# Keys, queries and attention outputs turned by DMA transposes instead of TensorE, in a fused attention and feed-forward kernel

## The chip, the cores and the metric

The kernel runs on one core of a Trainium2 chip. The core has a matrix engine (TensorE, PE in the profile, with its weight loads as PEld), a vector engine (DVE), a scalar engine (ACT), a general engine (POOL), a queue processor that issues most of the transfers (SP), and 16 DMA engines that carry them. The metric is the device time of one execution in microseconds, and the time of a kernel is the median of its runs.

## What is computed

Inputs are float32: `q`, `k`, `v` of shape (8 batches, 8 heads, 576 tokens, 64), 16 "beacon" keys and values for each batch and head that stand ahead of the others, and two weight matrices of 512 x 2048 and 2048 x 512. The reference, cut to what matters:

```python
k_all = np.concatenate([beacon_k, k], axis=2)          # 592 keys
v_all = np.concatenate([beacon_v, v], axis=2)
scores = scale * np.matmul(q, k_all.transpose(0, 1, 3, 2))
causal[:, Nb:] = np.triu(np.ones((S, S), dtype=bool), k=1)   # beacons are always seen
a = softmax(np.where(causal, -1e9, scores))
attn_out = np.matmul(a, v_all)                          # (B, H, S, D)
x = attn_out.transpose(0, 2, 1, 3).reshape(B * S, H * D)     # 4608 x 512
h = x @ w_in
g = np.where(h > 0.0, h, np.exp(np.minimum(h, 0.0)) - 1.0)   # elu
out = g @ w_out                                         # 4608 x 512, float32
```

## The kernel before

**Attention** runs batch by batch and, within a batch, over four pairs of heads (`n` counts pairs, 32 in all). Keys and queries of a pair come from HBM as one tile `st32` (L266): a partition holds nine consecutive tokens of one head, keys on the even partitions and queries on the odd ones, so that a row of the transfer is 9 x 64 floats. POOL or DVE casts the tile to bfloat16 (`cast_pair`, L275). The matmul needs the 64 features on the partitions, so TensorE turns the tile with nine transposes of 128 x 128 and one for the beacon keys (`do_T`, L310) into the PSUM tile `tr`, which shares the two buffers of tag `sc` with the scores. DVE copies the keys out of it in token order (`do_kT`, L322) and ACT or DVE the queries (`do_qT`, L327).

Scores are made transposed, keys on the partitions (`do_SC`, L334), in chunks of 128 keys (`NKC`, 5) and three ranges of queries (0 to 240, 240 to 496, 496 to 576; `CUT`, L183). The last range is padded so that its last chunk is 128 columns wide (L168). ACT takes the exponential (`do_exp`, L346), POOL masks the diagonal parts (`do_mask`), TensorE multiplies with `v` (`do_AV`, L364), and DVE divides by the row sum (`do_norm`, L380), which gives `x16`, tokens on the partitions. The feed-forward needs x with its 512 columns on the partitions: TensorE transposes each pair's five blocks (`do_xT`, L395), and DVE copies the result to `xT` (`do_xcopy`, L404).

**The feed-forward** runs over tiles of 512 tokens (the first is cut in two): 16 first matmul steps (`do_mm1`, L418: `hps`), elu over ACT (`do_e`), POOL (`do_clamp`) and DVE (`do_join`, giving `gt`), 16 second steps (`do_mm2`, L445: `ops`), a copy `osb` on DVE and a store. Each step is four matmuls of 128 x 512. A tile needs the x of all the batches that its tokens come from.

**Loads.** SP issues nearly all of them. `v` comes by tokens, 128 tokens on the partitions and rows of 64 floats (L280), and is cast by DVE into `v16`. Weights come in 32 pieces through buffers of tag `gt`, which later hold the elu's results.

**The order.** `Plan` (L27) is a list scheduler that runs when the kernel is built. Each operation has an engine, a key (its due time), an assumed duration, the operations it depends on and the buffers it takes and gives back. The planner goes through time and starts on each engine the ready operation with the smallest key; on TensorE none that is due more than 16 us after the earliest one left. Instructions are written in that order, so on the chip each engine's order is fixed and only the waits move. `place(b, a)` (L477) gives the due times of batch b with 32 us from one batch to the next; `SHIFT`, `AT`, `AT0`, `PACES`, `LAG` and `URGE` are hand-set due times, `FIRST` the order of the first loads, `ON_POOL` and `Q_ON_ACT` say which engine casts and copies. SP's loads are chained one behind the other in key order (L639); stores take their place by due time.

Of the kernel before, what the change touches and what calls it, by code (L numbers as in the profile page):

```python
# [27 lines left out]

# [85 lines left out]
def kernel(  # L119
# [43 lines left out]
    class Cut:  # L163
        def __init__(self, ranges, splits):
            self.ranges, self.parts, self.units, self.of_range = ranges, [], [], []
            for (lo, hi), split in zip(ranges, splits):
                part = [(jc, max(lo, first_q[jc]), hi - max(lo, first_q[jc])) for jc in range(NKC) if first_q[jc] < hi]
                if hi == S:  # L168
                    part[-1] = (part[-1][0], part[-1][1], P)
                self.parts.append(part)  # L170
                self.of_range.append(list(range(len(self.units), len(self.units) + len(split))))
                for chunks in split:
                    self.units.append([p for p in part if p[0] in chunks])
# [14 lines left out]
    SQP = BLOCKS[-1][0] + P  # L188
# [20 lines left out]
    NG, NET, NKQ = 20, 8, 4  # L209
# [16 lines left out]
    xT = [big.tile([P, NT], FP16, name=f"xT{cc}") for cc in range(NCC)]  # L226
# [4 lines left out]
    kTs = [big.tile([P, SKP], BF16, name=f"kT_{i}") for i in range(NKQ)]  # L231
    qTs = [big.tile([P, SQP], BF16, name=f"qT_{i}") for i in range(NKQ)]
# [3 lines left out]
    with tc.tile_pool(name="psum", bufs=1, space=bass.MemoryType.PSUM) as psum:  # L236
        slots = {
            "sc": 2, "ff": 4, "av": 2, "ops": 1, "et": NET, "rl": 2, "e": NE, "gt": NG, "osb": 3,
            "st": 4, "sb": 2, "bk": 1, "vst": 5,
# [14 lines left out]
        issues = []  # L254

        bks = {}

        def load_bk(b):
            t = bks[b] = stage.tile([P, DM], FP32, tag="bk", name="bk32", bufs=1)
            nc.sync.dma_start(  # L260
                out=t[0:NB].rearrange("n (h d) -> n h d", h=H), in_=beacon_k[b].rearrange("h n d -> n h d"))
# [17 lines left out]

        def load_v(b, jc):  # L280
            vst = vsts[b, jc] = stage.tile([P, H, D], FP32, tag="vst", name="vst", bufs=5)
# [28 lines left out]
        def do_T(n):  # L310
            b, hp = divmod(n, HP)
            tr = trs[n] = psum.tile([P, 2 * 1024], BF16, tag="sc", name="tr", bufs=2)
            for g in range(G):
# [3 lines left out]
                out=tr[:, P * G:P * G + NB], in_=bk16s[b % 2][0:NB, P * hp:P * hp + P], identity=identb[0:NB, 0:NB])  # L317
# [9 lines left out]
        def do_qT(n, eng):  # L327
            out, in_ = qTs[n % NKQ][:, 0:S].rearrange("c (p g) -> c p g", g=G), in_order(n, 1)
            if eng is nc.scalar:
                eng.activation(out=out, in_=in_, func=AFT.Copy)  # L330
            else:
                eng.tensor_copy(out=out, in_=in_)
# [14 lines left out]
        def do_exp(n, u):  # L347
            w = CUT.width[u]
            et = ets[n, u] = attn.tile([P, 2, 512], FP16, tag="et", name="et", bufs=NET)
# [12 lines left out]
        def do_AV(n, groups):  # L362
# [3 lines left out]
            for i, blk in enumerate(blocks_of(groups)):  # L366
                q0, rows, nk = BLOCKS[blk]
                for h in range(2):
                    c = (2 * i + h) * VW
                    for jc in range(nk):  # L370
# [8 lines left out]
                            start=(jc == 0), stop=(jc == nk - 1), skip_group_check=True)  # L379
            avs[n, groups[0]] = av  # L380
# [77 lines left out]
        def do_store(tt, t4):  # L458
# [5 lines left out]
        SHIFT = [3.37, -1.96, 6.24, 4.57, 2.84, -4.23, 2.71, 5.78]  # L464
        AT = [6.55, -0.8, -0.58, -0.4, -1.02, 0.94, 2.18]
        AT0 = [[-30.36, -35.31, -37.63, -37.29], [-37.9, -27.04, -33.24, -32.64], [-16.09, -15.68, -1.02, 2.44]]
        PACES = [(-17.79, 2.03, 18.97, 2.42), (-2.78, 3.03, 40.86, 0.57), (35.62, 1.7, 18.91, 3.41), (71.48, 2.79, 36.3, 3.28), (111.77, 1.64, 28.1, 2.06)]
        ON_POOL = ("1101011100110100", "1111111110110110", "01001010")
        LAG = 20.58
        URGE = 13.63  # L470
        Q_ON_ACT = "11111110"
        FIRST = (
            "k0 q0 b0 q1 i3 v0 k1 q2 k3 v2 i8 k2 q3 v1 v3 i0 i7 i4 i11 i15 i10 v4 i9 i2 i5 i1 i13 b1 k4 "
            "i6 i14 q4 i12 v5 o2 o5 o3 o8 o0 o6 o7 v6 q5 k5 o1 o4 o9 v9 k6 v8 q6 o12 v7 o14 o10 q7 o11 "
            "o15 o13 k7 ").split()
# [6 lines left out]
        scaled, last_xT = {}, {}  # L482
# [8 lines left out]
        def plan_loads(n):  # L491
            b, hp = divmod(n, HP)
            if hp == 0:
                got = load(load_key(f"b{b}", place(b, 0) - 31), 0.2, partial(load_bk, b), take=["bk"])
                bk_in[b] = add("POOL", place(b, -0.9), 0.6, partial(cast_bk, b),
                               deps=[got, last_T.get(b - 2)], give=["bk"])
# [11 lines left out]
        def plan_v(b):  # L508
            for jc in range(NKC):
                key = load_key(f"v{NKC * b + jc}", place(b - 1, 1.8 + 0.4 * jc))  # L510
                got = load(key, 1.25, partial(load_v, b, jc), take=["vst"], issue=1.0 if jc == 0 else 0.5)
# [9 lines left out]
        def plan_pair(n):  # L521
# [3 lines left out]
            T = add("PE", key, 0.6, partial(do_T, n),  # L525
# [4 lines left out]
            if Q_ON_ACT[b] == "1":  # L530
                qT = add("ACT", key + 0.4 - URGE, 0.7, partial(do_qT, n, nc.scalar), deps=[T, last_kq.get(n - NKQ)])
            else:
                qT = add("DVE", key + 0.5 - URGE, 0.77, partial(do_qT, n, nc.vector), deps=[T, last_kq.get(n - NKQ)])
            add("NONE", key, 0.0, None, deps=[kT, qT], give=["sc"], lat=0.0)
            masked = {}
# [3 lines left out]
            for units, key in steps:  # L539
                SC = add(  # L540
                    "PE", key, sum(0.00024 * 2 * CUT.width[u] + 0.02 for u in units), partial(do_SC, n, units),
                    deps=[kT, qT, SC], take=["sc"] * len(units), mode=1, lat=0.19)
                last_kq[n] = SC
# [12 lines left out]
            for r, groups in enumerate([(0,), (1,), (2,)] if b == 0 else [(0,), (1, 2)]):  # L556
# [10 lines left out]
                    deps=[AV, last_xT.get(n - 2 * HP)], give=["ff", "av"]))  # L567
                if b and r == 0:
                    continue
                if b:  # L570
                    groups, key = (0, 1, 2), at(AT[6])
                blks = blocks_of(groups)
# [11 lines left out]
        def plan_tile(p):  # L584
# [3 lines left out]
            for b in range(B):  # L588
                for r, (rlo, rhi) in enumerate(CUT.ranges):
                    if b * S + rlo < hi and b * S + rhi > lo:  # L590
                        xs += [scaled[b * HP + hp, r] for hp in range(HP)]
# [31 lines left out]
        for t in kTs:  # L623
            nc.vector.memset(t[:, SK:SKP], 0.0)
        for t in qTs:
            nc.vector.memset(t[:, S:SQP], 0.0)
# [5 lines left out]
        for b in range(B):  # L632
            plan_v(b)
            for hp in range(HP):
                plan_loads(b * HP + hp)
# [35 lines left out]
```

## Time and profile before

| | |
|---|---|
| median of 3 runs | 378.2 us (376.53 to 382.88) |
| profiled execution | 377.09 us, its span 375.4 us |
| granted TensorE clock | 0.999 |
| TensorE busy | 355.5 us |
| DVE, ACT, POOL busy | 231.7, 205.5, 199.9 us |
| HBM read and written | 37.22 and 9.44 MB |

The profile is one execution. The span runs from its first to its last instruction; the execution's own time is 1.7 us longer. The busy time of an engine is the sum of its instructions' durations without overlap. Matmuls are pipelined, and their ends are modelled: two neighbours overlap in the rows of the timeline, and the start of one to the start of the next is what a step takes. In the lists a row names the engine, the line of the kernel (L314), the operation, what it writes and reads, and the count. "SPq" rows are DMA issues on SP's queue; a DMA row gives the size and the median time from issue to landing.

Where the change is made, the page counts these operations: 288 transposes of keys and queries (L314) and 32 of beacon keys (L316) on TensorE; 32 key copies (L324) of 756 ns in the mean and 32 small ones (L325) of 156 on DVE; 28 query copies on ACT (L330) of 650 ns and four on DVE (L332) of 748; 160 transposes of x (L400) on TensorE, and 40 copies of x (L407) on DVE, of which 28 are 128 x 576 at 455 ns; 27 casts of pairs on POOL (L277) at 1148 ns and five on DVE at 808.

### The profile page before, as it was taken

The page shows a single profiled execution, that of the slowest core. Times are in us where ns is not written, and L with a number is a line of the kernel's source. Part 1 is how long each engine was busy: PE and PEld are TensorE (multiplying, and loading weights), DVE is VectorE, ACT ScalarE, POOL GpSimd, SP SyncE. Part 2 cuts the span into 40 slices and gives each one's busy share as a digit, 9 for nine tenths or more (in the row PEclk, how much of TensorE's full clock was granted, in tenths as well). Part 3 has the DMA queues.
Part 4 walks back from the last instruction along what each step waited for, and adds up shares of the span by engine and source line. Part 5 has one row for each costly group of instructions (what it writes and reads, how often), then busy time and mean ns, then how long its engine had stood idle before and what let it go on. Part 6 is the DMA issues. An engine that isn't in the chain of part 4 may idle for free.

```text
span 375.4 us, 8560 instructions
## 1 busy us (share of the span) xinstructions
PE 355.5 (95%) x3360; PEld 199.7 (53%) x3360; DVE 231.7 (62%) x489; ACT 205.5 (55%) x301; POOL 199.9 (53%) x369
## 2 busy tenths in 40 slices
PE   1598999999999999999999999999999999999995
PEld 1367766645556555555655455554655544444442
DVE  2469798668657867668847645666765645555321
ACT  2566767568857767887654455655563333333100
POOL 3459998467846755766744535546343333433200
PEclk9999999999999999999999999999999999999999
DMA  7999999992363467293272420000000000100021
GB/s 186 277 324 322 298 314 248 318 246 93 92 174 100 141 151 177 86 255 97 66 203 74 110 75 30 30 28 30 31 31 28 30 28 28 56 30 28 30 91 76
DMA packets 58855, 47.21 MB, mean 126 GB/s; under 512 B 41920, under 2 KB 41920, under 8 KB 58816
## 3 DMA queue, kind: packets, MB, share of 16 engines
q1 hardware_dynamic: 58672, 46.38, 43.1%
q8 instruction: 26, 0.43, 0.5%
q10 hardware_dynamic: 144, 0.29, 0.2%
q14 instruction: 13, 0.11, 0.1%
HBM read 37.22 MB, written 9.44 MB: 124 GB/s over the span
## 4 chain that ended last, share of the span: by engine, by line
PE 81%; DMA 8%; SPq 3%; DVE 3%; POOL 2%; ACT 1%; issue 1%; ACTq 0%; DVEq 0%
PE ops L450 32%; PE hps L423 30%; PE av L375 6%; PE sc L341 6%; DMA wst<-in_moe_w_in_dram 4%; DMA vst<-in_v_dram 3%; PE tr L314 3%; PE xt L400 2%; SPq L300 1%; DMA st<-in_q_dram 1%; POOL w_out L305 1%; POOL e L433 1%; DVE gt L442 1%; PE tr L316 1%; SPq L287 1%
## 5 line engine op out<-in xcount | busy, mean ns | idle before, releaser
L450 PE MATMUL ops<-w_out,gt 128*128 128x512 f16 x576 | 144.4, 379 | 0.0
L423 PE MATMUL hps<-xT,w_in 128*128 128x512 f16 (+1 forms) x640 | 143.7, 358 | 0.1
L433 POOL TENSOR_SCALAR e<-e 128x512 f32<-128x512 f32 x144 | 89.2, 621 | 98.6 <-ACT e L429 97.9
L429 ACT ACTIVATE e<-hps 128x512 f32<-128x512 f32 x144 | 85.8, 600 | 92.5 <-PE hps L423 89.2
L442 DVE SCALAR_TENSOR_TENSOR gt<-e,hps 128x512 f16<-128x512 f32 x144 | 97.5, 683 | 59.4 <-POOL e L433 58.8
L350 ACT ACTIVATE et<-sc 128x736 f16<-128x736 f32 (+3 forms) x128 | 106.2, 884 | 23.0 <-PE sc L341 21.8
L423 PEld LDWEIGHTS <-w_in 128*128 128x128 f16 x640 | 59.1, 98 | 55.5 <-issue 1.4
L450 PEld LDWEIGHTS <-gt 128*128 128x128 f16 x576 | 51.8, 98 | 57.3 <-issue 2.7
L356 POOL TENSOR_SCALAR_AFFINE_SELECT et<-et 128x256 f16<-128x256 f16 (+2 forms) x160 | 60.8, 401 | 37.0 <-ACT et L350 34.4
L375 PEld LDWEIGHTS <-et 128*128 128x128 f16 (+1 forms) x960 | 37.1, 99 | 12.0 <-issue 3.5
L341 PE MATMUL sc<-qT,kT 64*128 64x80 bf16 (+3 forms) x704 | 37.9, 238 | 5.7 <-ACT qT L330 3.9
L375 PE MATMUL av<-v,et 128*128 128x65 f16 (+1 forms) x960 | 41.9, 195 | 1.0 <-DVE v L291 0.7
L456 DVE COPY osb<-ops 128x512 f32<-128x512 f32 x36 | 24.8, 689 | 24.3 <-PE ops L450 24.0
L324 DVE COPY kT<-tr 128x576 bf16<-128x576 bf16 x32 | 24.2, 756 | 19.2 <-PE tr L316 13.0
L277 POOL CAST st<-st 128x1152 bf16<-128x1152 f32 x27 | 31.0, 1148 | 8.5 <-PE tr L314 4.7
L330 ACT ACTIVATE qT<-tr 128x576 bf16<-128x576 bf16 x28 | 18.2, 650 | 29.1 <-DVE kT L325 18.1
L390 DVE TENSOR_TENSOR x<-av,rl 128x256 f16<-128x256 f32 (+2 forms) x68 | 32.1, 472 | 2.3
L341 PEld LDWEIGHTS <-kT 64*128 64x128 bf16 x704 | 22.0, 96 | 21.4 <-issue 10.6
L314 PE MATMUL tr<-identb,st 128*128 128x128 bf16 x288 | 23.2, 230 | 7.5 <-DVE st L277 6.0
L291 DVE CAST v<-vst 128x512 f16<-128x512 f32 (+1 forms) x40 | 22.2, 564 | 7.3 <-DMA vst<-in_v_dram 7.3
L314 PEld LDWEIGHTS <-st 128*128 128x128 bf16 x288 | 19.6, 103 | 12.9 <-DVE st L277 6.4
L389 DVE RECIPROCAL rl<-av 128x4 f32<-128x4 f32 (+2 forms) x68 | 12.4, 182 | 14.8 <-PE av L375 14.6
(25 smaller groups left out, 92.9 us busy)
## 6 DMA issues: line engine op xcount, KB each, us to landing
st<-in_k_dram SPq DMA_DIRECT2D x32, 288.0 KB, 3.5
out_dram<-osb SPq DMA_DIRECT2D x36, 256.0 KB, 2.0
st<-in_q_dram SPq DMA_DIRECT2D x31, 288.0 KB, 4.3
vst<-in_v_dram SPq DMA_DIRECT2D x24, 256.0 KB, 5.9
wst<-in_moe_w_in_dram SPq DMA_DIRECT2D x16, 256.0 KB, 6.6
wst<-in_moe_w_out_dram SPq DMA_DIRECT2D x16, 256.0 KB, 5.9
vst<-in_v_dram SPq DMA_DIRECT2D x8, 224.0 KB, 4.8
vst<-in_v_dram SPq DMA_DIRECT2D x8, 160.0 KB, 4.9
```

The source lines that it names most:

```text
L277: eng.tensor_copy(out=o.rearrange("p g h d -> p h g d"), in_=f32s[n].rearrange("p h (g d) -> p h g d", g=G))
L314: nc.tensor.transpose(out=tr[:, P * g:P * g + P], in_=b16s[n][:, g].rearrange("p h d -> p (h d)"), identity=identb)
L341: nc.tensor.matmul(out=sc[:, h, o:o + w], lhsT=kT[D * h:D * h + D, P * jc:P * jc + P], rhs=qT[D * h:D * h + D, q0:q0 + w], start=True, sto ...
L350: nc.scalar.activation(out=et[:, :, 0:w], in_=scs[n, u][:, :, 0:w], func=AFT.Exp, bias=0.0, scale=float(1.0 / (D ** 0.5)))
L356: nc.gpsimd.affine_select(out=et[:, :, c0:c0 + dw], in_=et[:, :, c0:c0 + dw], compare_op=ALU.is_ge, fill=fill0, base=q0 + NB - P * jc, pat ...
L375: nc.tensor.matmul(out=av[:, c:c + D + 1], lhsT=ets[n, CUT.unit_of[jc, at]][0:m, h, col:col + P], rhs=v16[0:m, jc, 2 * hp + h, 0:D + 1], s ...
L390: nc.vector.tensor_tensor(out=x16s[b % 2][:, blks[0]:blks[0] + nb, P * hp:P * hp + P].rearrange("q i (h d) -> q i h d", d=D), in0=av[:, :, ...
L423: nc.tensor.matmul(out=hps[:, (hi - lo) * j:(hi - lo) * (j + 1)], lhsT=w_in16[:, cc, P * fc:P * fc + P], rhs=xT[cc][:, lo:hi], start=(cc = ...
L429: nc.scalar.activation(out=e, in_=hpss[tt, i], func=AFT.Exp, bias=0.0, scale=1.0)
L433: nc.gpsimd.tensor_scalar(out=e, in0=e, scalar1=1.0, scalar2=0.0, op0=ALU.min, op1=ALU.max)
L442: nc.vector.scalar_tensor_tensor(out=gt, in0=es[tt, i], scalar=1.0, in1=hpss[tt, i], op0=ALU.subtract, op1=ALU.max)
L450: nc.tensor.matmul(out=ops, lhsT=gts[tt, fc][:, P * t4:P * (t4 + 1)], rhs=w_out16[:, fc, :], start=(fc == 0), stop=(fc == NFC - 1))
```

## The change

From batch 2 on (`PE_B = 2`) the path of keys and queries is another. `load_tok` loads them by tokens, as `v` is loaded: 128 tokens on the partitions, all eight heads in a row of 512, rows of the transfer 64 floats long; the beacon keys go ahead of chunk 0 of the keys. Two chunks share a buffer of tag `st`. `cast_tok` casts one or two chunks to bfloat16 on DVE or POOL, by the table `TOK`. `turn_tok` is a DMA transpose issued by SP, from the cast chunk in SBUF straight to the key or query tiles of all four pairs of heads, ten for each batch. These tiles are now one per batch and side, with two batches held (`kTa`, `qTa`). The scores of a pair wait for all ten transposes of their batch. TensorE's transposes, the copies from PSUM and the loads by pairs stay for batches 0 and 1.

For batches 1 to 7, x goes another way too: when all four pairs of a batch have a block of tokens in `x16`, `turn_x` transposes the block by DMA into `xT`, five for each batch. Batch 0 stays with TensorE and DVE.

Besides: the last range of scores isn't padded (its last chunk is 80 columns wide), and the eight `et` tiles are fixed buffers whose tail is cleared once by POOL; beacon keys are transposed with 128 rows; `v` staging has four buffers instead of five, shared with the beacon keys; the `gt` tag has 18 buffers instead of 20; more weight casts are on DVE; and due times, `FIRST` and the engine tables have new values.

```diff
-    NG, NET, NKQ = 20, 8, 4
+    NG, NET, NKQ = 18, 8, 2 * HP
+    PE_B = 2
...
-    kTs = [big.tile([P, SKP], BF16, name=f"kT_{i}") for i in range(NKQ)]
-    qTs = [big.tile([P, SQP], BF16, name=f"qT_{i}") for i in range(NKQ)]
+    kTa = [big.tile([P, HP, SKP], BF16, name=f"kT_{i}") for i in range(2)]
+    qTa = [big.tile([P, HP, S], BF16, name=f"qT_{i}") for i in range(2)]
...
+        TURN = 1.2
...
+        def load_tok(b, is_k, c):
+            if (b, is_k, c // 2) not in f32s:
+                f32s[b, is_k, c // 2] = stage.tile([P, 2, G * D], FP32, tag="st", name="st32", bufs=4)
...
+            nc.sync.dma_start(out=t[r0:r0 + n], in_=(k if is_k else q)[b, :, lo:lo + n, :].rearrange("h s d -> s h d"))
+
+        def cast_tok(b, is_k, c, m, eng):
+            o = b16s[b, is_k, c // 2] = stage.tile([P, G, 2, D], BF16, tag="sb", name="st16", bufs=2)
...
+        def turn_tok(b, is_k, c):
+            r0, n, lo = rows_of(is_k, c)
+            t = (kTa if is_k else qTa)[b % 2]
+            nc.sync.dma_start_transpose(
+                out=t[:, :, P * c:P * c + r0 + n],
+                in_=b16s[b, is_k, c // 2].rearrange("p g h d -> p (g h d)")[0:r0 + n, DM * (c % 2):DM * (c % 2) + DM])
+
+        def turn_x(b, blk):
+            q0, rows, _ = BLOCKS[blk]
+            nc.sync.dma_start_transpose(
+                out=xTa[:, :, b * S + q0:b * S + q0 + rows], in_=x16s[b % 2][0:rows, blk, :])
...
+        DMA_AT = [-22.53, -24.72, -12.02]
+        TOK = ("101010", "001000", "000101", "100000", "000111", "111110")
...
+        def plan_tok(b):
+            turned[b] = []
+            for is_k in (True, False):
+                for c in range(0, NKC, 2):
...
+                    for j in range(m):
+                        s = add("SP", place(b, DMA_AT[1]) + i, TURN, partial(turn_tok, b, is_k, c + j),
+                                deps=[cast, last_SC.get(b - 2)])
+                        turned[b].append(add("DMA", place(b, DMA_AT[1]) + i, 0.5, None, deps=[s],
+                                             give=["sb"] if j == m - 1 else [], lat=2.2))
...
+            ready = plan_copies(n) if b < PE_B else turned[b]
...
+                if b:
+                    for blk in blks:
+                        part.setdefault(blk, []).append(normed[-1])
+                    if hp == HP - 1:
+                        for blk in blks:
+                            s = add("SP", at(DMA_AT[2]), TURN, partial(turn_x, b, blk), deps=part.pop(blk))
```

## The prediction

> **What bounds the kernel now.** First the page's busy table, then the busy time by stretches, to see which engine leaves no gap, and where.
>
> ```profile
> PE 355.5 (95%) x3360; PEld 199.7 (53%) x3360; DVE 231.7 (62%) x489; ACT 205.5 (55%) x301; POOL 199.9 (53%) x369
> 0.00:36.00 36.00, 22.16 (x284) 16.84 (x285) 20.23 (x65) 18.70 (x25) 19.77 (x42) 1.00 0.97 274
> 36.00:60.00 24.00, 22.28 (x289) 16.43 (x287) 20.61 (x45) 17.30 (x28) 22.73 (x42) 1.00 1.08 291
> 60.00:371.00 311.00, 310.93 (x2791) 166.41 (x2789) 190.19 (x381) 169.55 (x251) 157.35 (x287) 1.00 0.33 96
> ```
>
> The first two numbers of a stretch are its bounds and length; then come the busy times of PE, PEld, DVE, ACT and POOL, the granted clock, the DMA share and GB/s. TensorE idles 13.8 us before 36 us, 1.7 us up to 60 us, and 0.07 us in the next 311. The clock is full. So from 60 us on the time is TensorE's own work, and each step taken out of it shortens the run if nothing arrives late. DMA is full only up to 80 us; behind 60 us it has a share of 0.33.
>
> A busy matmul row overlaps its neighbours, so I price a step by the distance from its start to the start of the next one, in TensorE's timeline:
>
> ```profile
> 59.34 1.03 PE L450 MATMUL ops<-w_out,gt 128*128 128x512 f16 x4
> 60.20 0.67 PE L314 MATMUL tr<-identb,st 128*128 128x128 bf16 x9
> 60.80 0.18 PE L316 MATMUL tr<-identb,bk 16*128 16x16 bf16 x1
> 60.91 1.05 PE L423 MATMUL hps<-xT,w_in 128*128 128x256 f16 x8
> ...
> 72.48 0.42 PE L400 MATMUL xt<-identh,x 112*128 112x112 f16 x5
> 72.74 1.03 PE L450 MATMUL ops<-w_out,gt 128*128 128x512 f16 x4
> ```
>
> A pair's key and query transposes hold TensorE from 60.20 to 60.91, 0.71 us (0.70 to 0.71 at the others I looked at); its x transposes from 72.48 to 72.74, 0.26 us.
>
> **What goes from TensorE.** Batches 2 to 7 have 24 pairs: 24 x 0.71 = 17.0 us. Batches 1 to 7 have 28 pairs with x transposes: 28 x 0.26 = 7.3 us. The last range of scores becomes 80 columns wide instead of 128 in one chunk; a scores step of 880 columns takes 0.48 us (277.64 to 278.13), so 48 columns are 0.03 us, 0.8 us over 32 pairs. Sum: 25.1 us. The eight beacon transposes that stay grow from 16 to 128 rows; the step around them takes 0.11 us now, and I bound the change by that, 8 x 0.11 = 0.9 us either way, and take nothing.
>
> **What goes from the others.** DVE loses 24 kT copies (0.756 + 0.156 us), four qT copies (0.748), 28 xT copies (0.45) and five casts of pairs (0.81): 41.5 us. ACT loses 20 qT copies (0.65) and 32 x 96 elements of exp (1024 against 736 elements differ by 0.242 us, so 0.08 us each): 15.6 us. POOL loses 27 casts of pairs (31.0 us in all) and gets eight back (1.148 each), loses six beacon casts (0.753) and eight weight casts (0.66). Casts by tokens come in: a pair's cast of 1152 elements takes 1.148 us on POOL and 0.81 on DVE, so a chunk of 512 takes 0.51 or 0.36. The new table puts 25 chunks on POOL (12.8 us) and 35 on DVE (12.6 us); DVE also gets the eight weight casts (0.65 each). Net: DVE 208 us, ACT 190, POOL about 182 (with a few small memsets), all under 60% of a 350 us run. None of them becomes the bound.
>
> **What comes in: the queue and the DMA.** These carry the change. SP's issues and the landings in the trace:
>
> ```profile
> 141.29 3.42 SPq L287 DMA_DIRECT2D vst<-in_v_dram x3
> vst<-in_v_dram SPq DMA_DIRECT2D x24, 256.0 KB, 5.9
> out_dram<-osb SPq DMA_DIRECT2D x36, 256.0 KB, 2.0
> 130.00:132.00 2.00, 2.00 (x23) 1.16 (x21) 1.93 (x6) 1.10 (x2) 1.14 (x1) 1.00 1.01 368
> 144.00:146.00 2.00, 2.00 (x40) 1.39 (x38) 1.51 (x4) 1.55 (x3) 1.21 (x4) 1.00 1.12 243
> ```
>
> Loads by tokens have the form of the v loads: rows of 256 bytes, where the pairs have runs of 2304. With a pair landing, a full DMA moves 368 GB/s (130 to 132 us); with v landing, 243 (144 to 146). A batch's keys and queries, 2.36 MB, thus take 9.7 us of DMA instead of 6.4. The v load's issue is 0.58 us in the median and 3.42/3 = 1.14 us when the queue is full.
>
> No row shows a DMA transpose. There are 6 x 10 of keys and queries and 7 x 5 of x, 95, each of 128 x 512 two-byte elements (128 KB). **Issue on SP:** not under a v load's 0.58 us, not over four pair issues, one for each block of 128 columns, 4 x 0.61 = 2.4 us. I take 1.2, the geometric middle; the order is written with the same 1.2, so beyond it loads run late against the plan. **DMA time:** at least 128 KB at 368 GB/s, 0.36 us; at most a whole v landing, 5.9 us, if they pass one at a time. I take 0.54 us, 128 KB at the 243 GB/s of 256-byte rows, the nearest row, and 2 us more to landing, as the stores show.
>
> The Trainium skill has two prices here. "VectorE: DVE Perf Modes", § The three transpose paths, gives the DMA crossbar 1309 ns for a 128x128 block and TensorE 390, and its rules send such a block to TensorE; four blocks would be 5.2 us, an estimate by that page and near my upper end. "DMA: Bandwidth & Descriptors", § Latency and other measured facts, gives 261 GB/s, so 0.50 us, near the value I took. The trace speaks against using the first as a rate: TensorE takes 0.71 us for ten blocks here, not ten times 390 ns.
>
> **Does it fit?** Batch 2's loads are issued from 52 us on (SP's timeline). Batch 7's first scores start at 249 us; a span 25 us shorter wants them a little sooner, but the feed-forward backlog gives some back: tiles 7 and 8 need batch 7's x, and 64 steps of 0.864 us plus 4 us at the end must follow it. So six batches have 198 us, 33 us each. SP per batch: 11 key and query loads and 6 v loads at 0.58, 4.5 stores at 0.37, 15 transposes at 1.2: 6.4 + 3.5 + 1.7 + 18 = 29.6 us. DMA per batch: 9.7 + 5 (v) + 3.2 (stores) + 15 x 0.54 = 26 us. Both fit, SP with only 3.4 us to spare.
>
> **New waits.** A transpose waits on SP for its cast, or for all four pairs' x. Behind it stand the next loads and the output stores. Loads are keyed some 30 us ahead, and three output buffers cover stores that come about every 8 us, so a few us are hidden; an SP blocked for over 20 us would hold output buffers, then the PSUM tile and TensorE. The first scores of a batch now need its whole batch of keys and queries, not one pair. For batch 2 that is tight: from 52 us, key and query loads (9.7 us) and v loads (5 us) through a full DMA end at about 67 us, the last transposes at about 72; TensorE first turns batch 2 at 67.85 now. I put 3 us of stall there. The fifth v buffer goes: DVE waited 7.3 us in all for v with five, TensorE 0.7 for those casts; with four I add nothing, at most 3 us. The changed start (other order of loads, 18 staging buffers instead of 20) moves the same bytes through a full DMA; of its 13.8 us of idle I let 3 us go either way and take none.
>
> **Sum.** The profiled execution is 377.1 us, its span 375.4. 377.1 - 25.1 + 3 = 355.0; the median of the three runs shown, 378.2, lies 1.1 above the profiled one, so **356 us**.
>
> **Rivals.**
> *Readiness (20%):* casts, transposes and loads wait for one another on SP, and each of six batches starts its scores 2 to 4 us late, with no filler in the written order. For it: SP has 3.4 us to spare, and TensorE's order is fixed. Against it: the trace has TensorE without gaps though DVE waits for v. Price: 12 to 24 us back: 365 to 377, likeliest 368.
> *Slow transposes (18%), slower than before:* SP is the bound if an issue is much over 1.2 us. Above (33 - 11.6)/15 = 1.43 us each 0.1 us costs 6 x 15 x 0.1 = 9 us; the gain is gone at 1.7 us, 2% slower follows from 1.8. At four pair issues, 2.4 us, it is 0.97 x 90 = 87 us, less the gain, so about 440. The same comes of a DMA time above 1.0 us, where 15 of them fill what 18 us of other traffic leave of 33. For it: no row excludes it. Against it: a v load's 1024 rows cost SP no more than a pair's 128. The Trainium skill's 1309 ns a block would put the time beyond this: 15 x 5.2 = 78 us of DMA a batch, well over 500 in all.
> *The end set by something else (7%):* the elu chain ACT, POOL, DVE, which the list of waits shows starved by TensorE (POOL waits 97.9 us for ACT, ACT 89.2 for TensorE), paces the steps once TensorE has less to fill in: 370 to 380, no change. Against it: each of the three is under 60% busy.
>
> **Chances.** Forecast 55% (348 to 366), the others as given. 2%, about what a measurement here can tell from no change, is 370.6 and 385.8. Faster: 55 + 13 (the readiness case below 370.6) = 68%. Same: 7 + 7 = 14%. Slower: 18%. The range leaves out the slow transposes: 346 (the forecast with 3 us won at the start, and the small costs at their lower ends) to 382.
>
> **What would show it.** TensorE's key and query transposes end with batch 1 and its x transposes with batch 0; TensorE is near 330 us busy; idle after 60 us under 5 us; SP's transposes at 1.2 us or less and landing within 3 us. Wrong if TensorE waits before scores for the key and query tiles, or before the first feed-forward matmul for x, or if SP's timeline is filled from 50 to 250 us.

## The result, and the profile after

The changed kernel takes 400.85 us (median of four runs) against 378.62 for the kernel before: 1.060 times as long, with a 95% interval of 1.054 to 1.066. The prediction was 356 us, so it was wrong in sign. The profiled execution of the changed kernel takes 400.19 us, its span is 398.5.

The busy table and the busy time by stretches of the changed kernel (bounds, length, then PE, PEld, DVE, ACT, POOL, granted clock, DMA share, GB/s):

```profile
PE 343.6 (86%) x2980; PEld 181.2 (45%) x2980; DVE 206.0 (52%) x427; ACT 190.8 (48%) x281; POOL 185.1 (46%) x361
0.00:36.00 36.00, 19.54 (x234) 14.09 (x234) 18.47 (x55) 16.00 (x20) 20.41 (x50) 0.84 1.00 296
36.00:60.00 24.00, 20.79 (x241) 15.58 (x241) 17.88 (x43) 14.86 (x23) 19.01 (x31) 0.88 1.03 262
60.00:260.00 200.00, 168.47 (x1610) 86.86 (x1609) 104.05 (x217) 105.09 (x155) 96.76 (x190) 0.96 0.82 163
260.00:395.00 135.00, 134.79 (x900) 64.65 (x898) 65.12 (x114) 54.87 (x85) 48.91 (x92) 1.00 0.23 62
```

Between 60 and 260 us TensorE, which had no gap before, now waits 31.5 us, and the DMA share has gone to 0.82. Behind 260 us it is full again. The clock is no longer full: 0.96 in the middle stretch and less before. TensorE's last instruction ends at 394.8 us instead of 371.1. The 23.7 us between them split as follows: 35.6 us more idle time (2.6 before 36 us, 1.5 up to 60, 31.5 up to 260), and 11.9 us less busy time. I had counted on 25.1 us less; the other 13.2 came back as slower matmuls (below).

The queue is where the change shows. From the key tiles' list and the list of DMA issues (the column behind the count is median landing; min/median/max of the issue in ns in the first row):

```profile
L307 SPq DMA_TRANSPOSE kT<-st x30: 1174/1210/2403, 64.3 to 263.4; - x30
...
DMA to landing us min/median/max: 2.3/3.2/4.9
```

```profile
xT<-x SPq DMA_TRANSPOSE x35, 2.5
kT<-st SPq DMA_TRANSPOSE x30, 3.2
qT<-st SPq DMA_TRANSPOSE x30, 2.6
```

A DMA transpose issues in 1.2 us and lands 2.5 to 3.2 us after the start of its issue (medians), as the prediction took it. Summed from SP's timeline, the issues take 186.3 of the 200 us between 60 and 260 us (67.4 before), and the gaps between them of over 0.2 us come to 0.9 us in all. SP is full.

One stall in the timeline shows the chain:

```profile
77.00 0.56 DVE L427 TENSOR_TENSOR x<-av,rl 128x384 f16<-128x384 f32 x1
...
78.51 0.61 POOL L300 CAST st<-st 80x512 bf16<-80x512 f32 x1 [1.92 <-DMA kT<-st]
80.23 2.52 SPq L313 DMA_TRANSPOSE xT<-x  x2
81.55 0.42 DVE L300 CAST st<-st 64x512 bf16<-64x512 f32 x1 [3.40 <-DMA qT<-st]
...
82.85 1.20 SPq L307 DMA_TRANSPOSE kT<-st  x1
84.14 1.20 SPq L307 DMA_TRANSPOSE qT<-st  x1
85.39 3.86 SPq L313 DMA_TRANSPOSE xT<-x  x3
...
89.45 3.14 PE L460 MATMUL hps<-xT,w_in 128*128 128x512 f16 x7 [5.50 <-DMA xT<-x]
```

The last division of batch 1 ends at 77.6 us. SP is then turning batch 2's queries; it issues two transposes of x at 80.2, two of batch 2 at 82.9 and 84.1, and the last three of x from 85.4. The casts wait meanwhile, for the transposes to give back the two cast buffers. TensorE stands for 5.5 us until x has landed. And the seven matmuls that follow take 3.14 us, about 0.43 us each, where four of the kernel before took 0.86: half the clock (the granted clock is 0.50 from 89.4 to 92.6 us).

Across batches: the last transpose of keys and queries is issued at 84.1, 118.8, 161.2, 197.8, 234.6 and 271.1 us for batches 2 to 7, one batch in 37.4 us. The first scores of batches 3 to 5 start within 1 to 3 us of them (122.0, 162.2, 199.8): those batches keep step with the transposes. Batch 7's scores begin at 288 us, well behind its transposes; there TensorE's own order sets the time again.

Between 60 and 260 us TensorE does not stand still at the scores: no wait over 0.15 us comes before one. The list of waits shows where the queue reaches it (who waited for what: us in total, times, longest):

```profile
POOL st L300 <- DMA kT<-st: 12.7, 5, 4.1
DVE st L300 <- DMA kT<-st: 10.8, 5, 4.8
DVE st L300 <- DMA qT<-st: 9.6, 5, 3.4
PE hps L460 <- DMA xT<-x: 9.3, 3, 5.5
POOL st L300 <- DMA qT<-st: 7.0, 3, 3.2
```

For x itself TensorE waits 9.3 us, in three places. The casts (L300) wait 40.1 us for transposes, because a cast needs one of the two cast buffers and only the transposes of earlier chunks give one back. DVE and POOL work in the written order too, so the divisions, masks and elu steps behind such a cast are late. Sixteen waits of TensorE over 0.6 us make up 28.5 of the 31.5 us. Followed back in the trace, 9.3 us are for x, 14.5 stand behind a cast that had waited for a key or query transpose, 3.3 behind a cast that had waited for its load, and 1.4 behind neither. The longest of the second kind is at 185.6 us: DVE's cast at 184.3 had waited 4.83 us for a key transpose, the division that TensorE needed came next on DVE, and TensorE waited 4.30 us.

### The profile page after: what moved, and what is told of

The parts are those of the page before. It is cut to its first block, busy times and chain, and to the rows that moved or that the text cites. A ratio compares the mean times of both kernels' runs of the same rounds, so it can differ in the third digit from the quotient of the medians.

```text
span 398.5 us, 7862 instructions
## 1 busy us (share of the span) xinstructions
PE 343.6 (86%) x2980; PEld 181.2 (45%) x2980; DVE 206.0 (52%) x427; ACT 190.8 (48%) x281; POOL 185.1 (46%) x361
## 3 DMA queue, kind: packets, MB, share of 16 engines
q1 hardware_dynamic: 155216, 57.70, 63.9%
## 4 chain that ended last, share of the span: by engine, by line
PE 59%; DMA 15%; SPq 8%; DVE 7%; POOL 6%; ACT 2%; issue 2%; DVEq 0%; POOLq 0%; ACTq 0%
PE ops L487 26%; PE hps L460 22%; PE av L411 6%; SPq L313 4%; PE sc L377 4%; DMA qT<-st 4%; DMA kT<-st 3%; DMA st<-in_q_dram 3%; DMA st<-in_k_dram 2%; POOL et L392 2%; DMA vst<-in_v_dram 2%; DVE gt L479 2%; POOL e L470 2%; DMA wst<-in_moe_w_in_dram 1%; DVE st L300 1%
## 5 line engine op out<-in xcount | busy, mean ns | idle before, releaser
L460 PE MATMUL hps<-xT,w_in 128*128 128x512 f16 (+1 forms) x640 | 147.8, 368 | 16.7 <-DMA xT<-x 9.3
L470 POOL TENSOR_SCALAR e<-e 128x512 f32<-128x512 f32 x144 | 89.8, 627 | 118.8 <-ACT e L466 118.3
L479 DVE SCALAR_TENSOR_TENSOR gt<-e,hps 128x512 f16<-128x512 f32 x144 | 96.7, 683 | 80.2 <-POOL e L470 79.9
L386 ACT ACTIVATE et<-sc 128x736 f16<-128x736 f32 (+3 forms) x128 | 103.9, 863 | 39.3 <-PE sc L377 36.7
L460 PEld LDWEIGHTS <-w_in 128*128 128x128 f16 x640 | 61.6, 100 | 79.2 <-issue 22.0
L487 PEld LDWEIGHTS <-gt 128*128 128x128 f16 x576 | 53.2, 98 | 63.4 <-issue 6.2
L411 PE MATMUL av<-v,et 128*128 128x65 f16 (+1 forms) x960 | 44.2, 199 | 18.1 <-POOL et L392 7.5
L411 PEld LDWEIGHTS <-et 128*128 128x128 f16 (+1 forms) x960 | 38.7, 101 | 31.5 <-POOL et L392 9.0
L327 DVE CAST v<-vst 128x512 f16<-128x512 f32 (+1 forms) x40 | 18.3, 460 | 19.2 <-DMA vst<-in_v_dram 19.0
L300 POOL CAST st<-st 128x1024 bf16<-128x1024 f32 (+2 forms) x15 | 13.4, 892 | 30.3 <-DMA kT<-st 12.7
L300 DVE CAST st<-st 128x1024 bf16<-128x1024 f32 (+2 forms) x21 | 13.7, 650 | 22.9 <-DMA kT<-st 10.8
L350 PE MATMUL tr<-identb,st 128*128 128x128 bf16 x72 | 7.5, 271 | 11.0 <-POOL st L276 10.1
L366 ACT ACTIVATE qT<-tr 128x576 bf16<-128x576 bf16 x8 | 5.2, 648 | 13.6 <-DVE kT L361 10.7
L350 PEld LDWEIGHTS <-st 128*128 128x128 bf16 x72 | 6.2, 124 | 11.7 <-POOL st L276 10.7
```

The source lines that it names most:

```text
L300: eng.tensor_copy(out=o.rearrange("p g h d -> p (g h d)")[0:n, 0:DM * m], in_=f32s[b, is_k, c // 2].rearrange("p h f -> p (h f)")[0:n, 0:D ...
L386: nc.scalar.activation(out=et[:, :, 0:w], in_=scs[n, u][:, :, 0:w], func=AFT.Exp, bias=0.0, scale=float(1.0 / (D ** 0.5)))
L411: nc.tensor.matmul(out=av[:, c:c + D + 1], lhsT=ets[n, CUT.unit_of[jc, at]][0:m, h, col:col + P], rhs=v16[0:m, jc, 2 * hp + h, 0:D + 1], s ...
L460: nc.tensor.matmul(out=hps[:, (hi - lo) * j:(hi - lo) * (j + 1)], lhsT=w_in16[:, cc, P * fc:P * fc + P], rhs=xT[cc][:, lo:hi], start=(cc = ...
L470: nc.gpsimd.tensor_scalar(out=e, in0=e, scalar1=1.0, scalar2=0.0, op0=ALU.min, op1=ALU.max)
L479: nc.vector.scalar_tensor_tensor(out=gt, in0=es[tt, i], scalar=1.0, in1=hpss[tt, i], op0=ALU.subtract, op1=ALU.max)
```

## The experiments

The changed kernel is 401 us below; "SP" is the issue time between 60 and 260 us as summed above. The runs were spread over four chips. The number in parentheses behind a time is its ratio to the kernel before on the same chip, with the 95% interval; for the changed kernel it is 1.060 [1.054, 1.066].

### Each path alone, with the old due times

First a 2 x 2: the changed code with the due times, tables and load order of the kernel before, with each path taken back or not. Keys and queries go back by `PE_B = 8`; x goes back by the old branch in `plan_pair`:

```diff
-    PE_B = 2
+    PE_B = 8
...
-                            s = add("SP", at(DMA_AT[2]), TURN, partial(turn_x, b, blk), deps=part.pop(blk))
...
+                if b and r == 0:
+                    continue
+                if b:
+                    groups, key = (0, 1, 2), at(2.18)
+                blks = blocks_of(groups)
```

Both paths:

> The changed kernel with the due times, engine tables and load order of the kernel before (SHIFT, AT, AT0, PACES, ON_POOL, LAG, URGE, FIRST, Q_ON_ACT); both DMA paths stay. Theory A, the full SP queue (transposes of keys and queries, token loads, x transposes and stores one behind the other in one queue): the times matter little, 395 to 410 us, with TensorE idle for over 25 us behind 60 us. Rival B, the new due times are what loses: near 360 us, TensorE without gaps.

Keys and queries alone:

> As the run with both paths and the old times, but x goes through TensorE and DVE as before (35 DMA transposes fewer, about 42 us of SP). Theory A: the x transposes no longer stand behind keys and queries, SP has some 6 us a batch more, so part of the loss goes: 375 to 390. Rival B: 378 - 17 = 361. Rival C, x is the only thing that comes late: below 370.

x alone:

> As the run with both paths and the old times, but keys and queries of all batches go by pairs through TensorE as before; only x of batches 1 to 7 is turned by DMA. Theory A: SP is far from full (21.9 us of 33 a batch less the token loads), so the 7.3 us of TensorE time come out: 369 to 375. Rival B: the same. Rival C, the x path itself is late (12 us behind the last division in the changed kernel's trace): over 380.

Neither:

> The changed kernel with neither DMA path and with the old times: left are the 80-column chunk, four buffers of v staging shared with the beacon keys, 18 buffers of tag gt and the cleared tiles. All theories: 375 to 382, the kernel before within 1%. If it is over 385, the small edits carry part of the loss.

| | us | ratio to before | SP of 200 us | TensorE busy of 200 us |
|---|---|---|---|---|
| neither | 377.7 | 0.998 [0.994, 1.003] | 66.4 | 199.2 |
| x | 379.1 | 0.999 [0.994, 1.004] | 103.6 | 193.1 |
| keys and queries | 390.5 | 1.031 [1.023, 1.038] | 164.8 | 180.1 |
| both | 407.1 | 1.074 [1.066, 1.083] | 184.1 | 166.7 |

The small edits alone make no difference. The new due times are not the loss: with the old ones it is larger (407 against 401). Keys and queries alone lose 12.8 us, x alone about 1.5, both together 29.4: 15 us more than the sum. What the two share is SP's queue and the DMA engines. The x path alone did not give back its 7.3 us either, though SP was half empty; theory A had missed that.

### What in the queue costs: the issues, the loads, or the written order

Token loads from ACT's queue:

```diff
-            nc.sync.dma_start(out=t[r0:r0 + n], in_=(k if is_k else q)[b, :, lo:lo + n, :].rearrange("h s d -> s h d"))
+            nc.scalar.dma_start(out=t[r0:r0 + n], in_=(k if is_k else q)[b, :, lo:lo + n, :].rearrange("h s d -> s h d"))
```

> The changed kernel with the token loads of keys and queries (66 with the beacon keys, 46 us of SP's 186 us of issue between 60 and 260 us) issued from ACT's queue; order and everything else are planned by the same due times. Theory A, SP's issue time is the bound (186 of 200 us): SP falls to about 140 us, the transposes come earlier, 375 to 390 us, although ACT now issues too. Rival D, the DMA engines and the 256-byte rows are the bound (share 0.82): no change, 397 to 405. Against both: if ACT's exponentials wait behind its loads, over 405.

It took 397.1 us (1.045 [1.037, 1.053]). SP fell to 138.3 us as expected, and the time by 4 us only. This row of the stretch from 60 to 260 us shows why that is no verdict on SP:

```profile
60.00:260.00 200.00, 180.73 (x1718) 95.01 (x1718) 112.28 (x230) 111.46 (x166) 104.49 (x202) 0.94 0.94 169
```

TensorE gained 12 us there (180.7 against 168.5), while the DMA share went to 0.94. Before 60 us it lost 6 (34.4 us busy instead of 40.3): ACT's exponentials at 50.6 and 55.5 us come after gaps of 4.0 and 3.4 us in which ACT issued loads (later up to 6.1 us at once).

Long rows from HBM:

```diff
-                in_=(k if is_k else q)[b, :, lo:lo + n, :].rearrange("h s d -> s h d"))
+                in_=(k if is_k else q)[b].rearrange("h s d -> (h s d)").rearrange("(r h d) -> r h d", h=H, d=D)[lo:lo + n])
```

> The changed kernel with as many token loads of the same bytes, but each reads rows of 2048 bytes instead of 256 from HBM (it reads tokens and heads mixed, so the scores are of other numbers; the work is the same). Rival D, DMA time: the loads land in 3 us instead of 4.6, the DMA share falls by 0.2, and the time falls by 10 us or more. Theory A: the issue of a load falls from 0.9 to about 0.6 us, 15 us less of SP in all, so 390 to 398; the transposes' 107 us stay.

378.4 us, 0.997 [0.992, 1.002] of the kernel before: 22 us of the loss are gone, far more than theory A gave it. The mean issue of such a load fell from 0.91 to 0.57 us, which over the 60 loads is 20 us of SP; the median landing hardly moved (4.6 to 4.5 us). TensorE was busy for 184.7 of the 200 us:

```profile
60.00:260.00 200.00, 184.71 (x1796) 95.93 (x1795) 117.49 (x243) 116.63 (x171) 107.08 (x210) 0.98 0.82 176
```

Rival D had the size right (10 us or more) but not its signs: the loads land as late as before, and the DMA share stayed 0.82, with more bytes moved in the same time (176 GB/s instead of 163). Over the whole run the time of the DMA queue fell too, by 16 us (63.4% of 376.7 us instead of 63.9% of 398.5). So this run shows that the short rows cost the time, but it does not separate their cost on SP from their cost on the DMA engines.

Order written with the measured prices:

```diff
-        TURN = 1.2
+        TURN = 1.35
...
-            return add("DMA", key, dur, None, deps=[issue], lat=2.0)
+            return add("DMA", key, dur, None, deps=[issue], lat=2.5)
...
-                    gots = [load(place(b, 0) - 30 + i + 0.01 * j, 1.25, partial(load_tok, b, is_k, c + j),
-                                 take=["st"] if j == 0 else [], issue=1.0 if is_k and c + j == 0 else 0.5) for j in range(m)]
+                    gots = [load(place(b, 0) - 30 + i + 0.01 * j, 1.5, partial(load_tok, b, is_k, c + j),
+                                 take=["st"] if j == 0 else [], issue=1.4 if is_k and c + j == 0 else 0.9) for j in range(m)]
```

(The store's price went from 0.47 to 0.75 as well.)

> The changed kernel, ordered with the prices that its trace shows (transposes 1.35 us instead of 1.2, token loads 0.9 instead of 0.5, stores 0.75 instead of 0.47, landings later); no instruction added or taken away. Rival E, the loss comes of an order written for too cheap a queue, not of the queue itself: below 390. Theory A: the queue is as full as before, 393 to 405.

396.6 us (1.044 [1.035, 1.053]); SP 188.3 us. Better prices with the same due times bring 4 us; the queue stays full.

Each transpose of keys and queries cut in two:

```diff
-            nc.sync.dma_start_transpose(
-                out=t[:, :, P * c:P * c + r0 + n],
-                in_=b16s[b, is_k, c // 2].rearrange("p g h d -> p (g h d)")[0:r0 + n, DM * (c % 2):DM * (c % 2) + DM])
+            for f in range(2):
+                nc.sync.dma_start_transpose(
+                    out=t[:, 2 * f:2 * f + 2, P * c:P * c + r0 + n],
+                    in_=b16s[b, is_k, c // 2].rearrange("p g h d -> p (g h d)")[0:r0 + n, DM * (c % 2) + 256 * f:DM * (c % 2) + 256 * f + 256])
```

> The changed kernel with each of the 60 transposes of keys and queries cut into two of 256 columns. If the issue on SP goes with the columns, each takes 0.6 to 0.7 us and the time stays within 397 to 405. If an issue costs 1.2 us whatever it moves, SP gets 72 us more; theory A then gives 440 to 470 us (12 us a batch); rival D, DMA time, still 397 to 405.

```profile
L308 SPq DMA_TRANSPOSE kT<-st x60: 1160/1200/2407, 64.1 to 335.9; - x60
```

```profile
60.00:260.00 200.00, 140.81 (x1244) 70.94 (x1243) 81.80 (x172) 83.35 (x123) 70.37 (x143) 0.86 0.59 122
```

474.6 us (1.251 [1.241, 1.262]), 74 us more for 60 issues more. The issue of 256 columns costs the same 1.20 us as that of 512, and the run grows by what SP gets: 60 x 1.2 = 72. The DMA share falls to 0.59, so here the issue is the bound, and not the DMA engines.

### Fewer issues

If an issue has a fixed price, two chunks of keys in one transpose should be cheaper. The key tiles get the chunk as an outer dimension, so that the output of 1024 columns is one block:

```diff
+                nc.sync.dma_start_transpose(
+                    out=kTm[b % 2][:, c:c + m, :, 0:n].rearrange("p c h t -> p (c h) t"),
+                    in_=b16s[b, is_k, c // 2].rearrange("p g h d -> p (g h d)")[0:n, 0:DM * m])
...
-                            lhsT=kT[D * h:D * h + D, P * jc:P * jc + P],
+                            lhsT=kT[D * h:D * h + D, P * jc:P * jc + P] if n < PE_B * HP else kTm[n // HP % 2][D * h:D * h + D, jc, n % HP],
```

> The changed kernel with the key tiles laid out so that two chunks of keys are turned by one DMA transpose of 1024 columns: three issues a batch for the keys instead of five, 12 fewer in all. If the issue costs 1.3 us whatever it moves (what halving the columns showed), SP is 16 us freer and theory A gives 401 - 16 = 385 us (380 to 391). If it goes with the columns from 512 on, or if the 256-byte loads alone set the pace, 396 to 405.

399.5 us (1.054 [1.046, 1.061]): nothing. The price is fixed: the merged transposes of chunks 2 and 3 issue in 1.24 to 1.27 us in five of the six batches (those of chunks 0 and 1 in 1.42 to 2.96; the single ones of the changed kernel take up to 2.40). But the time did not follow. What took the gain's place is seen in the stretch from 60 to 260 us, and in TensorE's longest stall behind 250 us with the two rows of DVE ahead of it:

```profile
60.00:260.00 200.00, 174.49 (x1690) 90.10 (x1689) 105.75 (x221) 112.43 (x164) 103.80 (x202) 0.96 0.92 171
```

```profile
261.20 0.42 DVE L301 CAST st<-st 64x512 bf16<-64x512 f32 x1 [7.80 <-DMA qT<-st]
261.55 0.68 DVE L499 COPY osb<-ops 128x512 f32<-128x512 f32 x1
262.28 2.25 PE L493 MATMUL ops<-w_out,gt 128*128 128x512 f16 x6 [4.22 <-DVE osb L499]
```

SP is as full as before (185.4 us), now with the DMA share at 0.92: one full resource behind the other. Batch 7's last key and query transpose comes 9.4 us sooner than in the changed kernel (261.7 against 271.1), its first scores only 1.4 us (286.7): on the way there TensorE waited 4.2 us for the copy of an output tile. That copy stood on DVE behind a cast for which DVE had been idle for 7.8 us, until a query transpose landed and gave a cast buffer back. No run had more than two cast buffers, so what more of them would bring is open.

Merged keys and long rows together, that is the last edit and this one:

```diff
-            nc.sync.dma_start(out=t[r0:r0 + n], in_=(k if is_k else q)[b, :, lo:lo + n, :].rearrange("h s d -> s h d"))
+            nc.sync.dma_start(out=t[r0:r0 + n], in_=(k if is_k else q)[b].rearrange("h s d -> (h s d)").rearrange("(r h d) -> r h d", h=H, d=D)[lo:lo + n])
```

> The changed kernel with merged key transposes and with token loads of 2048-byte rows (other numbers, the same work). The long rows alone gave 378.4. If SP's queue is one line in which issue-bound transposes and DMA-bound loads add up, 12 transposes fewer still count: 366 to 374. If the row length alone had set the pace: 376 to 381.

378.3 us (1.002 [0.997, 1.006]): the same as long rows alone. The last transposes are issued within 3.3 us of the first scores of batches 2 to 4, and 3.7, 6.6 and 23.4 us ahead of those of batches 5, 6 and 7, so keys and queries no longer set the pace behind batch 5. TensorE still waits 15.6 us in all behind 60 us, most of it before first feed-forward matmuls.

### The start

```diff
-        AT0 = [[-49.64, -54.47, -36.46, -44.6], [-31.39, -43.84, -39.54, -19.29], [-15.64, -36.93, -2.07, -13.98]]
+        AT0 = [[-30.36, -35.31, -37.63, -37.29], [-37.9, -27.04, -33.24, -32.64], [-16.09, -15.68, -1.02, 2.44]]
...
-            "i8 i7 b0 q1 k0 q0 k1 i4 i3 v2 k2 q2 v0 k3 v1 q3 i11 i15 i6 v3 i0 v4 o2 o7 i10 o3 o6 i1 q4 "
+            "k0 q0 b0 q1 i3 v0 k1 q2 k3 v2 i8 k2 q3 v1 v3 i0 i7 i4 i11 i15 i10 v4 i9 i2 i5 i1 i13 b1 k4 "
```

> The changed kernel with the load order FIRST and the due times AT0 of batch 0 from the kernel before; everything from batch 1 on as changed. If the loss of the start (TensorE first at 9.8 us, granted clock 0.59 to 0.73 between 20 and 40 us, about 13 us in all) goes through to the end: 385 to 392. If the queue sets the pace behind 60 us and swallows it: 397 to 405.

407.2 us (1.076 [1.066, 1.085]). It did not mend the start: TensorE is busy for 39.6 us of the first 60 and the clock is 0.80 from 36 to 60 us, so it doesn't answer the question. The run with both paths and the old times does better there (42.4 us busy, clock 1.00 up to 60 us) and ends later than the changed kernel. So a good start does not save the run; what the bad one costs stays open.

### From batch 4 on, and with due times chosen anew

```diff
-    PE_B = 2
+    PE_B = 4
```

> As the run with both paths and the old times, but keys and queries go by tokens and DMA transposes from batch 4 on instead of 2 (40 transposes and 44 token loads instead of 60 and 66; batches 2 and 3 stay with TensorE: 5.7 us more of its work). Theory A, SP's time between 60 and 260 us: about 20 x 1.3 + 22 x 0.9 - 16 x 0.65 = 35 us of SP less, so 407 - 35 = 372 us or where another bound stops it (372 to 388). If the loss comes once for each batch that waits for its whole keys and queries, a third of 29 us: 397.

389.9 us (1.029 [1.020, 1.038]), 17 us below both paths from batch 2 on, but not the 35 expected. SP is at 164.4 us.

Then the same instructions in another order: all due times and engine tables were chosen again by a random search that lowers the length of the plan, with the prices of the order experiment above (a token load at 0.8). The edit, with one of the new values:

```diff
-        DMA_AT = [-22.53, -24.72, -12.02]
+        DMA_AT = [-20.48, -107.36, -104.1]
```

(SHIFT, AT, AT0, PACES, ON_POOL, LAG, URGE, TOK and FIRST got new values in the same way.)

> As the last one, with due times and engine tables chosen anew for the prices of the changed kernel's trace (transposes 1.35 us, token loads 0.8, stores 0.75); transposes stand first on SP. Theory A: with SP under 85% full and the order knowing it, the TensorE time that went (12 us) mostly comes out: 365 to 376. If waits for keys, queries and x stay whatever the order: as the last one.

371.3 us (0.981 [0.975, 0.987]). SP is as full as in the run before (163.5 us), yet TensorE is busy for 192.7 us of the 200 instead of 178.2. With a fifth of SP free, an order that knows the queue hides most of the waits. But is it the DMA path that gains? The control is the kernel with neither path, reordered in the same way:

> The kernel with neither DMA path (377.7 with the old times), with due times chosen anew in the same way as for the version from batch 4 on. If new due times alone explain that version's 371: 368 to 373. If its gain is the TensorE time that went to the DMA: 374 to 380.

370.2 us (0.981 [0.974, 0.988]). The new due times alone explain the 371. With merged keys, and new due times for them:

> DMA transposes from batch 4 on, merged key transposes (8 fewer) and due times chosen anew. The version without merging gave 371.3 with SP 82% full between 60 and 260 us. If SP still counts there: 362 to 369. If the queue no longer sets the pace: 369 to 373.

369.0 us (0.977 [0.970, 0.983]): no clear difference from the control. It had 12.6 us less TensorE work but was 6.7 us behind at 60 us. So its other due times were chosen once more, with the load order, the batch-0 times and the weight-cast table of the control held fast:

> DMA transposes from batch 4 on with merged keys, and the load order, batch-0 due times and weight-cast table of the reordered kernel with neither path; the other due times chosen anew. If the late start ate the 12.6 us of TensorE work that the transposes take away: 360 to 366. If waits for keys, queries and x eat it: 367 to 372.

> Only x of batches 1 to 7 by DMA, with due times chosen anew (379.1 with the old times). SP has room (104 of 200 us with the old times), so the 7.3 us of TensorE time should come out against the reordered kernel with neither path: 362 to 367. If x comes late whatever the order: 369 to 374.

> The reordered kernel with neither path once more, for the comparison on one chip: 369 to 372 by all theories.

On one chip: 366.65 us (0.968 [0.962, 0.974]) from batch 4 on with merged keys and the better start; 372.7 (0.983 [0.977, 0.989]) for x alone by DMA; 371.2 (0.980 [0.974, 0.985]) for neither. The first lies between its two expectations. It is the fastest kernel of this study, 4.5 us below the control (its runs 364.0 to 368.5, the control's 370.2 to 372.6). The stretch from 60 to 260 us of that kernel and of the control:

```profile
60.00:260.00 200.00, 191.98 (x1966) 100.08 (x1958) 121.08 (x254) 126.38 (x185) 114.69 (x225) 1.00 0.82 169
```

```profile
60.00:260.00 200.00, 199.95 (x2134) 113.19 (x2132) 134.92 (x292) 128.34 (x191) 120.60 (x222) 1.00 0.45 126
```

TensorE's busy time over the run is 336.1 against 349.8 us, 13.7 us less, and 8 us are given back as waits in this stretch. x alone by DMA gains nothing over the control: TensorE is busy for 2.8 us less (347.0), and 3.5 us of waits come in behind 60 us. But none of these waits is for x: the longest, 2.1 us at 65.5 us, stands behind a weight cast on DVE. And TensorE starts at 9.6 us in this run, at 5.8 in the control, because the load order and the other times of batch 0 are new too. So the order found for this run may have eaten what the path gives; x alone with the control's start was not run. Whether new due times would also save the full change (from batch 2 on) was not tried on the chip.

## Why the prediction was wrong

**What TensorE loses** was right as work, wrong as time. Summed from start to start, waits left out, the transposes of keys, queries and beacons take 7.3 us instead of 24.9 and those of x 2.8 instead of 10.1: 24.9 us less, where the prediction had 24.3 for the two. But the feed-forward's matmuls take 9.4 us more in the same count (`hps` 133.1 instead of 126.6, `ops` 128.8 instead of 125.9) and those of `av` 3.7 more, for the same work. That term was missing from the sum: a wait of a few us is paid once as a wait and again in slower matmuls. The row at 89.45 us shows it at its clearest. Part of the term belongs to the changed start and not to the queue: before 60 us, where the idle time grew by only 4.1 us, the granted clock was 0.84 and 0.88. The Trainium skill, "TensorE: Matmul & The Clock Gate", § What's actually happening, states a gate that halves the clock after an idle window of about 3.4 us; the 5.5 us wait followed by matmuls at 0.43 us agrees.

**The other engines** were right: DVE 206 us (208 predicted), ACT 191 (190), POOL 185 (182).

**The transpose itself** was right: 1.2 us to issue, 2.5 to 3.2 us to land. Slow transposes as such were not what happened. The Trainium skill's 1309 ns ("VectorE: DVE Perf Modes", § The three transpose paths), taken for each block in turn, is not borne out: four blocks of 128 x 128 land in 2.4 us at the fastest, issue included.

**"Does it fit?"** is the step that failed. I summed 29.6 us of SP for a batch and had 33. With the same counts and the mean issue between 60 and 260 us: loads of keys and queries 11 x 0.875 = 9.6 (6.4 predicted), v loads 6 x 0.64 = 3.8 (3.5), stores 4.5 x 0.79 = 3.6 (1.7), transposes 15 x 1.32 = 19.8 (18), 36.8 us in all; the batches came at 37.4. (The stretch held fewer stores, 14, so what was issued in it comes to 186.3 / 200 x 37.4 = 34.8 us for a batch.) The term that was mis-sized most is the loads of short rows, which I priced at the median issue of an unhurried queue although I had quoted the 1.14 us of a full one further up. The long rows, which took 0.34 us from each, took 22 us from the run. I had treated SP's time and DMA's time as two sums that each fit; in one queue in order they add up, because a load that waits for the DMA engines holds up the transposes behind it, and a transpose that issues for 1.2 us keeps the engines short of work. That this is the mechanism is argued from these sums. Shown are its two ends: more issues cost their full price at a DMA share of 0.59, and fewer issues bring nothing at 0.92. How the full queue reaches TensorE is read from the trace, and my sum had no term for it: the casts hold DVE and POOL until transposes give back one of two buffers (14.5 of 28.5 us of TensorE's waits, x 9.3). Whether SP's issue, the DMA engines or the two buffers would bind last was not separated.

**The rivals.** Readiness named much of the mechanism (casts, transposes and loads waiting for one another on SP, SP with nothing to spare, no filler in the order), but put it at 12 to 24 us where 45 came back: 365 to 377 with 20%. It placed the waits at the scores, where TensorE has none, it left out the halved clock, and it took the lateness for 2 to 4 us a batch while it was 4.4 (37.4 - 33) and came with x on top. The rival for slower had the right place, SP, and the right way to price it (15 issues in the room that the others leave), but its point of decision, 1.43 us, was worked out with the cheap loads. With the measured ones it is (33 - 17.0) / 15 = 1.07 us, and the issue lay above it. The third, the elu chain, did not occur as written: POOL still waits for ACT and ACT for TensorE, and where TensorE waits for `gt`, most of the time a cast had held DVE or POOL.

**New waits.** That a full SP would hold output buffers and so TensorE was written down, but the wait that looks like it (4.2 us in the merged run) came from a cast on DVE. That a cast waits for the transposes ahead of it, and holds what stands behind it on its engine, was not written down. The 3 us for batch 2 was an order short of what came: 31.5 us of waits in the middle, spread over the batches and not in the first one. Of the three signs of being wrong two came: SP's timeline is full, and TensorE waits for x before the first feed-forward matmul. The third, a wait before scores, did not.

## What to carry to other kernels

Sum what an in-order queue must issue for each round of the loop, and price each issue as it is when the queue is full; a transfer waiting for its engines and an issue that is slow by itself add up in such a queue, even if each resource alone would fit. Look also for the small copies and casts that feed the queue: they sit in the order of another engine, and when their buffers are full they hold up work there that has nothing to do with the queue. Work taken from a bound engine is only worth its time while everything it waits for keeps ahead, and here a wait of 5.5 us also cost TensorE half its speed for 3 us more. Reorder the kernel without the change before crediting a reordered change: here new due times alone gave 7 us, and the DMA path 4.5 on top, from batch 4 on only.

## What the runs showed of the hardware that was not expected

- A DMA transpose from SBUF to SBUF issues in about 1.2 us on SP, whether it moves 256, 512 or 1024 columns (1.20, 1.21 and 1.24 to 1.27 us), and also with 64 or 80 rows instead of 128 (1.2 us). These are medians or undisturbed issues; single ones took up to 3.8 us.
- The same bytes in rows of 256 instead of 2048 bytes cost 0.34 us more of SP's issue for each load of 256 KB (0.91 against 0.57 in the mean between 60 and 260 us, at a DMA share of 0.82 in both runs), while the landing stayed the same (4.6 and 4.5 us).
- A transpose of 16 rows among those of 128 costs more than a full one. With the beacon keys padded to 128 rows, a pair's ten transposes hold TensorE for 0.56 us instead of 0.71 (168.50 to 169.06 in the rows below, of the reordered kernel with neither path; 60.20 to 60.91 in the kernel before), 3.8 us over the 25 pairs behind 60 us. The prediction gave this edit nothing. The Trainium skill, "TensorEngine Tiling (Array Packing)", § Key Properties, says that changing the tiling mode drains TensorE. The 0.15 us would fit it if a transpose of 16 rows changes the mode, which no run here shows.

```profile
168.50 0.67 PE L350 MATMUL tr<-identb,st 128*128 128x128 bf16 x9
169.01 0.22 PE L352 MATMUL tr<-identb,bk 128*128 128x128 bf16 x1
169.06 1.03 PE L460 MATMUL hps<-xT,w_in 128*128 128x512 f16 x4
```

- Matmuls of 512 columns behind a wait of 5.5 us ran at 0.43 us each instead of 0.22, at a granted clock of 0.50. Over the whole run the granted clock of the changed kernel was 0.957 (0.906 with the split transposes, 0.999 in the kernel before).
